# Moving the second MLP's weight tiles 96 bytes along each SBUF partition

## The chip, the cores and the metric

One core of one Trainium2 chip runs the whole program. The metric is the time of one execution on the device, in microseconds (us); the median of several runs is given. A profile is a record of one further execution; its span runs from its first to its last instruction.

## The reference

The input x has 12480 rows of 128 float32 values. The program computes an induced attention and two MLPs one behind the other:

```python
h = mab(inducing, x)          # softmax over 12480 keys, 32 inducing rows
x = mab(x, h)                 # each row of x attends to the 32 rows of h
t = x @ w_in1                 # 128 -> 2048
x = (t * np.cos(t)) @ w_out1  # 2048 -> 128
t = x @ w_in2
return (t * sigmoid(t)) @ w_out2
```

The four weight matrices come as float64 and are narrowed to float32 on the chip.

## The kernel before

A prologue (to 45 us of the span) reads x, computes h, and folds h into the first MLP's first weights: hw = h @ w_in1, so that mlp1_in takes the 32 attention weights of a row in place of the row. From there on a main loop treats 25 blocks, 22 of them of 512 rows of x, the last three of 480, 448 and 288. A block has NJ = 8 units, each of which covers two of the 16 slices of 128 of the hidden 2048.

The order of the work is written out by hand (manual_schedule): each engine executes its instructions in the order of the loop over steps s in main (line 739 on). In a step of the steady state TensorE gets 20 matmuls, of 128 x 128 weights and a moving tile of 512 columns:

- mlp1_in(s), line 761: 2 matmuls, weights hw, moving tile stk, into the PSUM tile h1.
- mlp2_in(s - 11), line 896: 6 matmuls. Weights and moving tile are split into two parts each, hi and lo, and the products wi2_0 x yhi, wi2_1 x yhi and wi2_0 x ylo are added up in the PSUM tile h2; so twice, for two slices.
- mlp2_out(s - 13), by way of down, line 843: 6 matmuls, wo2_0 x hi2 (two slices), wo2_1 x hi2 (two), wo2_0 x lo2 (two), into acc2.
- mlp1_out(s - 1), by way of down, line 843: 6 matmuls of the same form, with wo1_0, wo1_1, hi1 and lo1, into acc1.

So line 843 has the matmuls of both MLPs: in an ordinary step the first six are mlp2_out's and the next six mlp1_out's. In a few steps (held_back) mlp2_in moves behind mlp2_out or behind mlp1_out, since the scores of a later block (line 211) take its PSUM tile h2. The first 12 units of mlp1_out and the first 8 of mlp2_out use unsplit weights (line 853). Beside TensorE, ScalarE takes the cosine (796), the SiLU (911) and the hi part of its result (919), VectorE the product (800) and the parts hi1 and lo1 (807, 833), GpSimd the part lo2 (920).

Each weight tile is split once, in steps 4 to 15 (split, called in the loop): ScalarE writes the hi part (line 191), GpSimd the lo part (line 192). The second MLP's tiles wi2_0, wi2_1, wo2_0 and wo2_1, of 8192 bytes in each partition, come from the pool late, which is opened last (line 719 on), over space that the prologue has given back.

Where the tiles lie in a partition follows from the order and the sizes in which the pools are opened and the tiles asked for; each start is a multiple of 32 bytes. In the built program before:

| tile | first byte | remainder by 128 | remainder by 256 |
|---|---|---|---|
| hw0 to hw3 | 71392 to 77536 | 96 | 224 |
| wo1_0, wo1_1 | 79584, 87776 | 96 | 224 |
| stk | 96000 | 0 | 0 |
| hi1, lo1, hi2, lo2, yhi, ylo (all buffers) | 132992 to 192384 | 0 | 128 |
| wi2_0, wi2_1 | 196480, 204672 | 0 | 128 |
| wo2_0, wo2_1 | 212864, 221056 | 0 | 128 |

A partition ends at byte 229376. The dead tiles of the prologue under wi2 are win, pick, idle, the small ones behind them, e, et and, last, most (212768, 8 bytes); under wo2 there is none.

Of the kernel before, what the change touches and what calls it, by code (L numbers as in the profile page):

```python
# [9 lines left out]
F32 = mybir.dt.float32  # L10
# [12 lines left out]
def tile_induced_attention_then_two_mlps(  # L23
# [36 lines left out]
    P, G, Q = 128, 4, 32  # L60
# [658 lines left out]
    late = ctx.enter_context(tc.tile_pool(name="late", bufs=1, reuse_waits="tile"))  # L719
# [24 lines left out]
    def main(general):  # L744
# [3 lines left out]
        acc1, acc2 = {}, {}  # L748
        ast = {}
        pieces[:] = order[ahead:]  # L750
        wi2 = [late.tile([C, FF], F32R, name=f"wi2_{i}") for i in range(2)]
        wo2 = [late.tile([P, NF, C], F32R, name=f"wo2_{i}") for i in range(2)]
        pair_of.update(in2=wi2, out2=wo2)
# [315 lines left out]
    with tc.If(hot == 0) as arm:  # L1069
        main(False)  # L1070
    stacks = saved
    with arm.Else():
        main(True)
# [34 lines left out]
```

## Time and profile before

| | |
|---|---|
| median of 3 runs | 967.56 us (967.47 to 968.73) |
| profiled execution, its own time | 967.38 us |
| its span | 965.2 us |
| TensorE busy | 951.8 us, 4480 matmul records |
| VectorE busy | 779.3 us |
| ScalarE busy | 691.6 us |
| GpSimd busy | 517.2 us |
| matmuls of line 843 (both down functions) | 53% of the chain that ended last |
| matmuls of line 896 (mlp2_in) | 28% of it |

Busy TensorE means that a matmul was under way; the matmuls are pipelined, and their ends are modelled, so that one overlaps the next in the record. How fast they follow one another is read from their starts, or from differences of their mean durations.

### The profile page before, as it was taken

What the parts mean: (1) busy time and instruction counts of PE and PEld (TensorE: products, weight loads), DVE (VectorE), ACT (ScalarE), POOL (GpSimd) and SP (SyncE); (2) the same over time, 40 slices, a digit from 0 to 9 for tenths busy, and PEclk for the clock granted to TensorE, in tenths of its full rate; (3) what the DMA queues carried; (4) which work ended last, traced back from release to release, by engine and by line L of the source; (5) the groups of instructions that cost most, each with busy time, mean ns of one, the idle gap of its engine ahead of it and who ended that gap; (6) DMA issues with size and microseconds to landing.
All of it is one profiled execution on the core that took longest, in us unless ns stands there. A gap on an engine that the chain in (4) does not pass through costs nothing.

```text
span 965.2 us, 11951 instructions
## 1 busy us (share of the span) xinstructions
PE 951.8 (99%) x4480; PEld 758.0 (79%) x4481; DVE 779.3 (81%) x784; ACT 691.6 (72%) x725; POOL 517.2 (54%) x274
## 2 busy tenths in 40 slices
PE   8899999999999999999999999999999999999997
PEld 5456778888878888878888887888887888888896
DVE  4889888988887988888988887988888888878751
ACT  5687768777668776767777777777767777677774
POOL 3346545654545655554655544655455554555565
PEclk9999999999999999999999999999999999999999
DMA  9341000001010010010010010010010100100001
GB/s 356 112 138 45 6 18 11 14 20 22 2 22 12 12 22 12 12 22 12 12 22 12 12 22 12 12 22 7 17 22 1 22 14 9 21 12 5 13 11 20
DMA packets 65484, 28.19 MB, mean 29 GB/s; under 512 B 54440, under 2 KB 60040, under 8 KB 65416
## 3 DMA queue, kind: packets, MB, share of 16 engines
q1 hardware_dynamic: 64760, 27.24, 10.8%
q8 instruction: 37, 0.61, 0.3%
q14 instruction: 31, 0.25, 0.1%
q10 hardware_dynamic: 656, 0.09, 0.1%
HBM read 14.79 MB, written 6.39 MB: 22 GB/s over the span
## 4 chain that ended last, share of the span: by engine, by line
PE 95%; DMA 2%; DVE 1%; issue 0%; SPq 0%; ACT 0%; POOL 0%; ACTq 0%; POOLq 0%; DVEq 0%
PE acc L843 53%; PE h L896 28%; PE h L761 9%; PE acc L853 4%; DMA x_sb<-in_x_dram 2%; PE s L211 1%; PE pt L392 0%; PE hp L539 0%; SPq L328 0%; PE s L419 0%; DVE et L507 0%; DVE c L800 0%; DVE mx L432 0%; POOL lo L925 0%; PE misc L455 0%
## 5 line engine op out<-in xcount | busy, mean ns | idle before, releaser
L920 POOL TENSOR_TENSOR lo<-s,hi 128x1024 fp32r<-128x1024 f32 (+3 forms) x189 | 446.7, 2364 | 381.0 <-ACT hi L919 359.6
L843 PE MATMUL acc<-hi,wo 128*128 128x512 f32 (+3 forms) x1520 | 406.8, 389 | 0.0
L843 PEld LDWEIGHTS acc<-hi,wo 128*128 128x128 f32 x1520 | 282.5, 188 | 61.5 <-issue 3.7
L800 DVE TENSOR_TENSOR h<-h,c 128x1024 f32<-128x1024 f32 (+3 forms) x188 | 226.1, 1203 | 123.9 <-ACT c L796 123.7
L796 ACT ACTIVATE c<-h,half_pi 128x1024 f32<-128x1024 f32 (+3 forms) x200 | 219.2, 1096 | 146.9 <-PE h L761 146.1
L911 ACT ACTIVATE s<-h 128x1024 f32<-128x1024 f32 (+3 forms) x200 | 201.2, 1006 | 76.6 <-PE h L896 71.8
L896 PE MATMUL h<-yhi,wi 128*128 128x512 f32 (+3 forms) x800 | 244.2, 386 | 0.0
L843 PE MATMUL acc<-lo,wo 128*128 128x512 f32 (+3 forms) x760 | 232.6, 387 | 0.1
L807 DVE CAST hi<-h 128x1024 fp32r<-128x1024 f32 (+3 forms) x188 | 224.9, 1196 | 6.5
L833 DVE TENSOR_TENSOR lo<-h,hi 128x1024 fp32r<-128x1024 f32 (+3 forms) x188 | 223.9, 1191 | 5.7
L919 ACT CAST hi<-s 128x1024 fp32r<-128x1024 f32 (+3 forms) x189 | 195.3, 1033 | 6.1
L896 PEld LDWEIGHTS h<-yhi,wi 128*128 128x128 f32 x800 | 148.8, 188 | 30.7 <-issue 0.5
L843 PEld LDWEIGHTS acc<-lo,wo 128*128 128x128 f32 x760 | 141.9, 188 | 31.2 <-POOL lo L925 0.4
L896 PE MATMUL h<-ylo,wi 128*128 128x512 f32 (+3 forms) x400 | 154.3, 386 | 0.0
L761 PE MATMUL h<-stk,hw 128*128 128x512 f32 (+3 forms) x400 | 126.0, 396 | 1.4 <-ACT stk L704 0.7
L761 PEld LDWEIGHTS h<-stk,hw 128*128 128x128 f32 x400 | 74.1, 188 | 26.8 <-issue 6.5
L896 PEld LDWEIGHTS h<-ylo,wi 128*128 128x128 f32 x400 | 75.1, 188 | 15.2
L877 ACT CAST yhi<-acc 128x512 fp32r<-128x512 f32 (+3 forms) x25 | 14.4, 576 | 15.1 <-PE acc L843 15.0
L943 DVE STREAM_TRANSPOSE o<-acc 128x512 f32<-128x512 f32 (+3 forms) x25 | 17.3, 694 | 9.3 <-PE acc L843 9.3
L853 PE MATMUL acc<-c,wf 128*128 128x512 f32 x48 | 22.5, 591 | 0.0
L878 DVE TENSOR_TENSOR ylo<-acc,yhi 128x512 fp32r<-128x512 f32 (+3 forms) x25 | 16.7, 669 | 5.4 <-ACT yhi L877 5.3
L800 DVE TENSOR_TENSOR c<-h,c 128x1024 f32<-128x1024 f32 x12 | 14.6, 1216 | 2.4 <-ACT c L796 1.9
(133 smaller groups left out, 320.6 us busy)
## 6 DMA issues: line engine op xcount, KB each, us to landing
out_dram<-o SPq DMA_DIRECT2D x80, 64.0 KB, 1.9
x_sb<-in_x_dram SPq DMA_DIRECT2D x8, 512.0 KB, 9.2
raw<-in_moe_w_in_dram SPq DMA_DIRECT2D x8, 512.0 KB, 6.5
raw<-in_moe_w_out_dram SPq DMA_DIRECT2D x8, 512.0 KB, 4.5
stk<-ahi SPq DMA_DIRECT2D x40, 64.0 KB, 2.0
stk<-at SPq DMA_DIRECT2D x40, 64.0 KB, 2.0
x_sb<-in_x_dram SPq DMA_DIRECT2D x3, 256.0 KB, 3.7
x_sb<-in_x_dram SPq DMA_DIRECT2D x2, 320.0 KB
```

What stands on the lines that cost most here:

```text
L761: nc.tensor.matmul(ps[:, a, 0:n], lhsT=hw[f // 4][:, f % 4 * P : (f % 4 + 1) * P], rhs=stacks[b][:, 0:n], start=True, stop=True,)
L796: nc.scalar.activation(cs, h, AF.Sin, bias=half_pi, scale=1.0)
L800: nc.vector.tensor_tensor(cs if whole else h, h, cs, ALU.mult)
L807: nc.vector.tensor_copy(hi[:, :, 0:n], h)
L833: nc.vector.tensor_tensor(lo[:, :, 0:n], h, hi[:, :, 0:n].bitcast(F32), ALU.subtract)
L843: nc.tensor.matmul(acc[:, 0:n], lhsT=wt[:, 2 * j + a, :], rhs=gt[:, a, 0:n], start=(j == 0 and p == 0 and a == 0), stop=(j == NJ - 1 and p ...
L853: nc.tensor.matmul(acc[:, 0:n], lhsT=w[:, 2 * j + a, :], rhs=c[:, a, 0:n], start=(j == 0 and a == 0), stop=(j == NJ - 1 and a == 1),)
L896: nc.tensor.matmul(ps[:, a, 0:n], lhsT=wt[:, fs], rhs=yt[:, 0:n], start=(p == 0), stop=(p == 2),)
L911: nc.scalar.activation(sv, hid2.pop(u)[:, :, 0:n], AF.Silu)
L919: nc.scalar.copy(hv, sv)
L920: nc.gpsimd.tensor_tensor(lv, sv, hv.bitcast(F32), ALU.subtract)
L943: nc.vector.transpose(o.rearrange("p t d -> p (t d)")[:, 0:n], acc2.pop(b)[:, 0:n])
```

## The change

One tile of 24 float32, 96 bytes, that nothing reads or writes is asked of the pool late ahead of the four weight tiles:

```diff
         pieces[:] = order[ahead:]
+        late.tile([P, 24], F32, name="gap")
         wi2 = [late.tile([C, FF], F32R, name=f"wi2_{i}") for i in range(2)]
         wo2 = [late.tile([P, NF, C], F32R, name=f"wo2_{i}") for i in range(2)]
```

So wi2_0 starts at 196576, and the others 96 bytes further on as well: the remainder by 128 becomes 96 and that by 256 becomes 224, which are those of wo1 and hw. The last tile ends at 229344. Nothing else moves.

## Rows read from the trace of the kernel before

**Rows 1.** The page, parts 1 (busy us, share, instructions) and 4 (chain).
```profile
PE 951.8 (99%) x4480; PEld 758.0 (79%) x4481; DVE 779.3 (81%) x784; ACT 691.6 (72%) x725; POOL 517.2 (54%) x274
...
PE 95%; DMA 2%; DVE 1%; issue 0%; SPq 0%; ACT 0%; POOL 0%; ACTq 0%; POOLq 0%; DVEq 0%
```

**Rows 2.** The cores: span and mean granted TensorE clock.
```profile
core 0: 965.2 us, clock 0.998
```

**Rows 3.** Eight steps: stretch, its us, TensorE's busy time and matmuls, clock, DMA.
```profile
506.52:543.26 36.74, 36.74 (x161) 1.00 0.07 15
```

**Rows 4.** The timeline of one ordinary step: start, us, engine, line, operation.
```profile
511.11 0.62 PE L761 MATMUL h<-stk,hw 128*128 128x512 f32 x2
511.57 0.63 PE L896 MATMUL h<-yhi,wi 128*128 128x512 f32 x2
...
512.94 1.07 PE L843 MATMUL acc<-hi,wo 128*128 128x512 f32 x4
...
514.18 1.22 DVE L807 CAST hi<-h 128x1024 fp32r<-128x1024 f32 x1
...
514.30 1.10 PE L843 MATMUL acc<-hi,wo 128*128 128x512 f32 x4
...
515.71 0.39 PE L761 MATMUL h<-stk,hw 128*128 128x512 f32 x1
```

**Rows 5.** The listing by line, 508.74 to 509.6 us: mlp2_out (busy us, mean ns).
```profile
L843 PE MATMUL acc<-hi,wo 128*128 128x512 f32 x3 | 0.8, 389 | 0.0
L843 PE MATMUL acc<-lo,wo 128*128 128x512 f32 x2 | 0.6, 390 | 0.0
```

**Rows 6.** The same listing, 510.11 to 511.0 us: mlp1_out.
```profile
L843 PE MATMUL acc<-hi,wo 128*128 128x512 f32 x3 | 0.9, 398 | 0.0
L843 PE MATMUL acc<-lo,wo 128*128 128x512 f32 x2 | 0.6, 394 | 0.0
```

**Rows 7.** The same listing, 507.37 to 507.80 us: the first matmuls of mlp2_in.
```profile
L896 PE MATMUL h<-yhi,wi 128*128 128x512 f32 x2 | 0.8, 392 | 0.0
L896 PE MATMUL h<-ylo,wi 128*128 128x512 f32 x1 | 0.4, 393 | 0.0
```

**Rows 8.** The same listing, 508.0 to 508.1 us: later matmuls of mlp2_in.
```profile
L896 PE MATMUL h<-yhi,wi 128*128 128x512 f32 x2 | 0.6, 389 | 0.0
```

**Rows 9.** The timeline of a step whose mlp1_out is ahead of mlp2_in.
```profile
156.50 1.10 PE L843 MATMUL acc<-hi,wo 128*128 128x512 f32 x4
...
157.90 0.62 PE L896 MATMUL h<-yhi,wi 128*128 128x512 f32 x2
158.18 1.23 DVE L800 TENSOR_TENSOR h<-h,c 128x1024 f32<-128x1024 f32 x1 [2.16 <-ACT c L796]
...
159.27 0.39 PE L761 MATMUL h<-stk,hw 128*128 128x512 f32 x1
```

**Rows 10.** The listing by line, whole span: writes of wo2's (held) and wo1's (wf) hi parts.
```profile
L191 ACT CAST wo<-held 128x512 fp32r<-128x512 f32 x4 | 2.5, 617 | 0.0
L191 ACT CAST wo<-wf 128x512 fp32r<-128x512 f32 x4 | 2.4, 612 | 0.0
```

**Rows 11.** The listing by line and shape, whole span: matmuls of 512 columns.
```profile
L843 PE MATMUL acc<-hi,wo 128*128 128x512 f32 x1328 | 363.5, 395 | 0.0
L896 PE MATMUL h<-yhi,wi 128*128 128x512 f32 x704 | 219.0, 392 | 0.0
```

**Rows 12.** TensorE's timeline near the end: mlp1_out, then mlp2_out, of 448 columns.
```profile
895.84 0.98 PE L843 MATMUL acc<-hi,wo 128*128 128x448 f32 x4
...
897.08 0.57 PE L761 MATMUL h<-stk,hw 128*128 128x448 f32 x2
...
945.50 0.97 PE L843 MATMUL acc<-hi,wo 128*128 128x448 f32 x4
...
946.72 0.43 PE L896 MATMUL h<-yhi,wi 128*128 128x288 f32 x2
```

## The prediction

> **What bounds the kernel now.** I read the page first: TensorE is busy for 99% of the span, and the chain of waits that ended last lies on it for 95% [rows 1]. The granted clock is 0.998 of full speed, so 2.4 GHz throughout [rows 2]. Eight consecutive steps of the main loop, 160 matmuls, take 36.74 us and TensorE is busy in all of it [rows 3]. So in the main loop a nanosecond added to the spacing of the matmuls is a nanosecond of the run, and one saved there is saved until another engine's work becomes the longer; VectorE, the next, has 779.3 us in the span [rows 1]. The question is then only what sets the spacing of the matmuls.
>
> Next the timeline of one step [rows 4]. It has 20 matmuls of 512 columns: two of mlp1_in, six of mlp2_in, six of mlp2_out, six of mlp1_out. From start to start the groups take 511.57 - 511.11 = 0.46, 512.94 - 511.57 = 1.37, 514.30 - 512.94 = 1.36 and 515.71 - 514.30 = 1.41 us. mlp2_out and mlp1_out are the same function on the same shapes with the same kinds of operands, and yet one needs 0.05 us more. The listing by line, cut to those stretches, sharpens this. Its mean durations carry a modelled end, some 162 ns past the next start (389 ns beside 1.36 us / 6 = 227 ns), which drops out in differences. mlp2_out runs at 389 and 390 ns [rows 5], mlp1_out at 398 and 394 [rows 6]. mlp2_in runs at 392 and 393 in its first three matmuls [rows 7] and 389 after them [rows 8].
>
> What differs? The moving tiles (hi1, lo1, hi2, lo2, yhi, ylo) all start 0 bytes past a multiple of 128, and the second MLP's weights do too; wo1 and hw start 96 past one. The spacing follows the weights, not the moment: in the step from 154.59 us, in which the score work puts mlp1_out ahead of mlp2_in, mlp1_out again takes 157.90 - 156.50 = 1.40 us although VectorE had then stood idle for 2.16 us, and mlp2_in right behind it takes 159.27 - 157.90 = 1.37 us while VectorE works [rows 9]. In the ordinary step mlp1_out has VectorE beside it [rows 4]. Both times its price is the same. So neighbours on other engines don't make it.
>
> **The change, part by part.** *The unused tile.* It issues no instruction and no DMA, on no queue; no wait is added, so nothing is queued behind one. The four tiles still lie over the same dead tiles of the prologue (win to et, and most), so their first writers wait for the same releases. The last one ends 32 bytes below the end of a partition. Cost: zero; there is nothing that would need cover.
>
> *The writes of the moved tiles* (line 191 on ScalarE, line 192 on GpSimd). ScalarE writes to the tiles that move take 617 ns; those to wo1, which already lies at the new offset, take 612 [rows 10]. Eight such writes at a difference of -5 to +5 ns are 0.04 us, beside the matmuls. Zero.
>
> *The reads of the moved tiles by TensorE.* This is the whole price. After the change each matmul of the second MLP has weights 96 bytes past a multiple of 128 and a moving tile at 0, as mlp1_out has now. I take its rate. The two shown mlp1_out groups take 1.40 and 1.41 us, so 1.40 / 6 = 233 to 1.41 / 6 = 235 ns a matmul.
>
> - mlp2_out: from 389.4 to about 396.4 mean ns (three at 398 and two at 394 [rows 6] against three at 389 and two at 390 [rows 5]), that is 7 ns. Count: 1328 hi of 512 columns are listed under line 843 [rows 11], and by the code half as many lo, 664. mlp1_out has 164 units of six, 984, which leaves 1008. 1008 x 7 ns = 7.1 us.
> - mlp2_in: now (392.3 + 389) / 2 = 390.7; with the group's first matmul counted, mlp1_out has some 5 ns more (1.40 - 1.37 = 0.03 us in six). Count 704 yhi [rows 11] and half as many ylo: 1056 x 5 ns = 5.3 us.
> - The second mlp1_in matmul, behind which the first wi2 weights are loaded: no row by itself. Between 0 and 7 ns, 176 times, 0 to 1.2 us; I take the middle, 0.5.
> - Units of fewer columns: at 448, mlp1_out takes 897.08 - 895.84 = 1.24 us and mlp2_out 946.72 - 945.50 = 1.22 [rows 12], so 0.02 us a group, 16 groups, 0.3 us. Others: I take zero.
>
> Sum 7.1 + 5.3 + 0.5 + 0.3 = 13.2 us. The profiled execution took 967.38 us (span 965.2), 0.2 below the median of 967.56; 967.4 + 13.2 = **980.6 us**. All of it lies on the path, because TensorE has no idle time to give. No other engine is late next: they get 0.07 us more per step, and wait longer for TensorE.
>
> *Bounds.* Nearest from below: the moved weights cost only what the three unsettled matmuls of mlp2_in show, 392.3 mean ns [rows 7]. That is 2.9 x 1008 + 1.6 x 1056 = 4.6 us, 972.0. From above: all at 398, the slowest row of mlp1_out [rows 6], 8.6 x 1008 + 7.3 x 1056 = 16.4 us, with the small terms at 1.5 985.3. The middle is taken since it is the mean of the only group that has the new combination.
>
> **The rivals.** *No change (967.5 us).* The slow rate belongs to something of mlp1_out other than the address of its weights: its accumulator, acc1, lies in another PSUM bank than acc2. For it: each of the two groups has its own bank, and no row separates bank from weights. Against it: mlp2_in runs at both rates in the same bank h2 [rows 7, 8], and hw, at wo1's offset, writes h1, and its pair takes 0.46 us [rows 4], 230 ns each, above mlp2_out's 227. That the tiles don't move would also end here; the sizes (96 bytes, then four times 8192, pool opened last) speak against it.
>
> The Trainium skill, SBUF — State Buffer, section "SBUF: two separate sides", gives TensorE its own read ports, with a second independent one for the weights; by that rule the place of the weights is without effect and the time would stay at 967.5 us. The trace doesn't agree well. TensorE: Matmul & The Clock Gate, section "Back-to-back issue gap", gives 512 / 2.4 + 2.5, an estimate of 216 ns for such a matmul by itself; here they lie at 227 to 236, so weight loads and matmuls cost one another something.
>
> *Faster (about 959 us).* What is slow is not an offset but the change from one offset to another between successive weights, and after the change mlp2_in, mlp2_out and mlp1_out have one offset. It decides if a run of matmuls with equal offsets settles at 389 wherever that offset is. Then mlp1_out gets mlp2_out's rate, 0.04 us a step, and the first three of mlp2_in gain 3 x 3.3 ns, 0.01 us: 0.05 x 170 steps = 8.5 us. For it: mlp2_in is slow just behind mlp1_in and settles after three. Against it: mlp1_out doesn't settle within its six matmuls (the three behind its first run at 398, the two after them at 394 [rows 6]); and mlp2_in right behind mlp1_out needs no more than 1.37 us [rows 9], so a change of offset by itself isn't dear.
>
> **How the numbers follow.** Slower, as summed: 0.80. No change: 0.11. Faster: 0.09. A difference under 0.2% (1.9 us) can't be told from no change here. The forecast's own range is 972 to 986 and holds most of its 0.80; the range given reaches down to 967, so that it takes in the case of no change, and leaves out the faster case and the forecast's tails.
>
> **What would show it.** Right: mlp2_out at 395 to 398 mean ns in the listing by line, a step of 4.66 us or more instead of 4.59, mlp1_out unchanged at 394 to 398, the same number of instructions, and no new wait ahead of lines 191 and 192. Wrong: mlp2_out still at 389 (then it is the bank or the time), or mlp1_out at 389 too (then it was the change of offset). The size is wrong if six matmuls in a row are too few to show where a longer run at the new offset settles: then the rate changes along the 12 to 18 matmuls that come behind mlp1_in.

## The result, and the profile after

The changed kernel takes 981.34 us (median of 4 runs, 979.73 to 981.91) beside 967.67 us (967.47 to 968.73) for the one before: a ratio of 1.0139, 95% interval 1.0126 to 1.0152. The forecast was 980.6.

The page and the cores first; the line of part 1 answers to [rows 1], the core's to [rows 2]. The span here is that of the profiled execution, which took 981.91 us.

```profile
PE 965.3 (99%) x4481; PEld 760.4 (78%) x4481; DVE 779.8 (80%) x784; ACT 691.5 (71%) x725; POOL 517.2 (53%) x274
```
```profile
core 0: 979.7 us, clock 0.998
```

VectorE, ScalarE and GpSimd are busy for as long as before, to 0.5 us, with the same counts; the granted clock is the same. Only TensorE has more: 965.3 for 951.8 us. (One matmul record more is in the trace; the program has as many as before.) The time went into the spacing of the matmuls.

The timeline of one ordinary step, which answers to [rows 4]; lines stand one further down in the changed kernel.

```profile
514.06 0.63 PE L762 MATMUL h<-stk,hw 128*128 128x512 f32 x2
514.53 0.62 PE L897 MATMUL h<-yhi,wi 128*128 128x512 f32 x2
...
515.92 1.10 PE L844 MATMUL acc<-hi,wo 128*128 128x512 f32 x4
...
517.32 1.10 PE L844 MATMUL acc<-hi,wo 128*128 128x512 f32 x4
...
518.73 0.63 PE L762 MATMUL h<-stk,hw 128*128 128x512 f32 x2
```

From start to start: mlp1_in 0.47 us (before 0.46), mlp2_in 1.39 (1.37), mlp2_out 515.92 to 517.32, 1.40 (1.36), mlp1_out 1.41 (1.41, and 1.40 in [rows 9]). A step takes 4.67 us for 4.60. mlp2_out now runs as mlp1_out does.

The listing by line and shape over the whole span, matmuls of 512 columns (busy us, mean ns): after, and then the rows of before that did not stand ahead of the prediction.

```profile
L844 PE MATMUL acc<-hi,wo 128*128 128x512 f32 x1328 | 367.9, 399 | 0.0
L897 PE MATMUL h<-yhi,wi 128*128 128x512 f32 x704 | 221.4, 396 | 0.0
L844 PE MATMUL acc<-lo,wo 128*128 128x512 f32 x664 | 209.5, 397 | 0.0
L897 PE MATMUL h<-ylo,wi 128*128 128x512 f32 x352 | 139.7, 397 | 0.0
L762 PE MATMUL h<-stk,hw 128*128 128x512 f32 x352 | 114.7, 407 | 1.3 <-ACT stk L704 0.7 <-DVE c L801 0.6
```
```profile
L843 PE MATMUL acc<-lo,wo 128*128 128x512 f32 x664 | 206.8, 392 | 0.0
L896 PE MATMUL h<-ylo,wi 128*128 128x512 f32 x352 | 137.7, 391 | 0.0
L761 PE MATMUL h<-stk,hw 128*128 128x512 f32 x352 | 113.2, 403 | 1.4 <-ACT stk L704 0.7 <-DVE c L800 0.6
```

Less the busy times of [rows 11], 363.5 and 219.0 us, and of the rows above, that is 4.4 us (hi) and 2.7 (lo) for the two down functions, 2.4 and 2.0 for mlp2_in and 1.5 for mlp1_in: 13.0 us in all, with the same counts. The spans differ by 979.7 - 965.2 = 14.5. TensorE's timelines, before and then after, show where the rest lies: the first mlp1_in, and the last group of the run.

```profile
44.93 1.21 PE L761 MATMUL h<-stk,hw 128*128 128x512 f32 x4 [0.73 <-ACT stk L704]
...
957.79 0.82 PE L843 MATMUL acc<-lo,wo 128*128 128x288 f32 x2
```
```profile
45.73 0.72 PE L762 MATMUL h<-stk,hw 128*128 128x512 f32 x2 [0.73 <-ACT stk L704]
...
971.70 0.79 PE L844 MATMUL acc<-lo,wo 128*128 128x288 f32 x2
```

From one to the other it is 912.86 us before and 925.97 after, 13.1 us more, which the listing accounts for. 0.8 us lie ahead of it, where the prologue's transposes waited 1.3 us for x in place of 0.6, and 0.6 us behind it. The change touches neither, and the same program, run again with two tags traded (below), starts its first mlp1_in at 44.33 us.

### The profile page after: what moved, and what is told of

Same layout as the page of the kernel before. It is cut to its first block, busy times and chain, and to the rows that moved or that the text cites. A ratio compares the mean times of both kernels' runs of the same rounds, so it can differ in the third digit from the quotient of the medians.

```text
span 979.7 us, 11952 instructions
## 1 busy us (share of the span) xinstructions
PE 965.3 (99%) x4481; PEld 760.4 (78%) x4481; DVE 779.8 (80%) x784; ACT 691.5 (71%) x725; POOL 517.2 (53%) x274
## 4 chain that ended last, share of the span: by engine, by line
PE 96%; DMA 2%; DVE 1%; issue 0%; ACT 0%; SPq 0%; POOL 0%; ACTq 0%; POOLq 0%; DVEq 0%
PE acc L844 53%; PE h L897 28%; PE h L762 9%; PE acc L854 4%; DMA x_sb<-in_x_dram 2%; PE s L211 1%; PE hp L539 0%; PE pt L392 0%; PE s L419 0%; DVE et L507 0%; SPq L328 0%; DVE c L801 0%; DVE mx L432 0%; PE misc L455 0%; POOL lo L926 0%
## 5 line engine op out<-in xcount | busy, mean ns | idle before, releaser
L844 PE MATMUL acc<-hi,wo 128*128 128x512 f32 (+3 forms) x1520 | 411.2, 392 | 0.0
L844 PE MATMUL acc<-lo,wo 128*128 128x512 f32 (+3 forms) x760 | 235.2, 390 | 0.1
L897 PE MATMUL h<-ylo,wi 128*128 128x512 f32 (+3 forms) x400 | 156.3, 391 | 0.0
L392 PEld LDWEIGHTS pt<-ident,x_sb 128*128 128x128 f32 x98 | 11.2, 147 | 6.9 <-PE hp L539 3.1
```

The source lines that it names most:

```text
L844: nc.tensor.matmul(acc[:, 0:n], lhsT=wt[:, 2 * j + a, :], rhs=gt[:, a, 0:n], start=(j == 0 and p == 0 and a == 0), stop=(j == NJ - 1 and p ...
L897: nc.tensor.matmul(ps[:, a, 0:n], lhsT=wt[:, fs], rhs=yt[:, 0:n], start=(p == 0), stop=(p == 2),)
```

## The experiments

A tile's offset is its first byte's remainder by 256; the distance is the weights' offset less the moving tile's, again by 256. Before, the distance was 96 in mlp1_out, 224 in mlp1_in and 0 in the second MLP; the change made it 96 there too. In every kernel that follows the same arithmetic is done on the same values, and what differs, if anything, is places.

### The unused tile smaller

The edit of gap32, ahead of wi2:

```diff
+        late.tile([P, 8], F32, name="gap")
```

And that of gap64:

```diff
+        late.tile([P, 16], F32, name="gap")
```

> The second MLP's weights start 32 bytes past a multiple of 128, the moving tiles at 0. If the spacing follows the distance in bytes between weights and moving tile (my theory), 32 is another distance than 0 and 96; neither has a row yet. If any distance but 0 keeps the matmuls from settling, mlp2_out goes from 389 to about 396 mean ns and the run to 979 to 982 us, as at 96. If the slow rate is due to an accumulator's bank or to the moment, or if only 96 is slow, 967.5 us. If what matters is that all weights have one offset, this kernel has two, as before: 967.5 us as well.

> The second MLP's weights start 64 bytes past a multiple of 128. If the distance by 128 counts, slow as at 96, 979 to 982 us with mlp2_out near 396 mean ns. If only the place by 64 counts (wo1 and the changed tiles lie 32 past a multiple of 64, before none did), then 64 is as good as 0: 967.5 us and mlp2_out at 389.

Measured: gap32 978.60 us, ratio 1.0121 (1.0104 to 1.0138); gap64 977.09 us, 1.0098 (1.0081 to 1.0115). The listing by line of gap64:

```profile
L844 PE MATMUL acc<-hi,wo 128*128 128x512 f32 x1328 | 365.8, 397 | 0.0
L844 PE MATMUL acc<-lo,wo 128*128 128x512 f32 x664 | 208.9, 396 | 0.0
```

Both are slower than before, a little less than at 96 (397 and 396 ns here, 398 and 396 in gap32, against 399 and 397). gap32 came out 0.4 us and gap64 2 us under my lower end. So 96 is nothing special, and the place by 64 doesn't decide: a distance of 64 is dear as well.

### The first MLP's weights at a multiple of 256

```diff
+    flag = persist.tile([1, 1], I32, name="flag")
     hw = [persist.tile([P, FF // 4], F32R, name=f"hw{i}") for i in range(4)]
     wo1 = [persist.tile([P, NF, C], F32R, name=f"wo1_{i}") for i in range(2)]
-    flag = persist.tile([1, 1], I32, name="flag")
```

> The tile flag is asked for ahead of hw, so that hw and wo1 start at a multiple of 128 (and of 256), as the second MLP's weights do by 128; all else stays. My theory: mlp1_out drops from 396 to 389 mean ns, 984 matmuls by 6.7 ns = 6.6 us, the unsettled first three of mlp2_in 176 x 10 ns = 1.8 us and the second mlp1_in at most 1 us: 958 to 961 us. If a period of 256 counts, wo1 now stands at 128 from its moving tile by 256 and need not gain: 964 to 970. Bank or moment: 967.5, and mlp1_out stays at 396.

Measured: 973.50 us, ratio 1.0069 (1.0052 to 1.0086). No branch of the expectation held: it got slower. TensorE's timeline of one of its steps:

```profile
513.96 0.63 PE L761 MATMUL h<-stk,hw 128*128 128x512 f32 x2
514.43 0.64 PE L896 MATMUL h<-yhi,wi 128*128 128x512 f32 x2
...
515.83 1.08 PE L843 MATMUL acc<-hi,wo 128*128 128x512 f32 x4
...
517.21 1.10 PE L843 MATMUL acc<-hi,wo 128*128 128x512 f32 x4
...
518.60 0.63 PE L761 MATMUL h<-stk,hw 128*128 128x512 f32 x2
```

mlp1_out, from 517.21, takes 1.39 us, hardly less than the 1.40 to 1.41 of before. So a start at a multiple of 128 isn't what makes a tile fast, for wo1 has it now: its distance by 256 is 128. And mlp2_in rose from 1.37 to 1.40 us and mlp2_out from 1.36 to 1.38, although none of their tiles was moved. A matmul's rate therefore depends on more than its own two tiles. Over the 129 ordinary steps of this trace the matmuls come back to 227 ns from start to start only with the fourth of mlp2_out, so the reading is that the slow matmuls ahead of them in the stream cost them something.

### The accumulators' tags traded

```diff
-                acc1[b] = psa.tile([P, 512], F32, tag="acc1" if b else "acc2", name="acc1")
+                acc1[b] = psa.tile([P, 512], F32, tag="acc2" if b else "acc1", name="acc1")
...
-                acc2[b] = psa.tile([P, 512], F32, tag="acc2", name="acc2")
+                acc2[b] = psa.tile([P, 512], F32, tag="acc1", name="acc2")
```

> acc1 and acc2 trade their PSUM banks, no tile of the SBUF moves. My theory: no change, 967.5 us, mlp1_out at 396 and mlp2_out at 389 mean ns. If the bank makes the slow rate, the two trade their rates: mlp2_out 396, mlp1_out 389, and the sum stays about the same, so the rates decide and not the time.

The edit trades the tags under which acc1 and acc2 are asked for, and not the banks: in both built programs acc1 of the first block and every acc2 lie in bank 6 and acc1 of the later blocks in bank 7, and the two programs have the same instructions with the same addresses. So this is the kernel before, run again, and not the trade that the expectation speaks of.

Measured: 967.36 us, ratio 1.0000 (0.9991 to 1.0010). That is how closely two sets of runs of one program agree; it says nothing on the banks. The rival of the banks falls by other runs. With every accumulator where it was, the change took mlp2_out from 1.36 to 1.40 us, and all_at_128, which follows, takes mlp1_out from 1.40 to 1.36.

### Everything at one offset: 128, then 224

The edit of all_at_128:

```diff
+    flag = persist.tile([1, 1], I32, name="flag")
+    m2 = persist.tile([P, KT, 1], F32, name="m2")
+    sm = persist.tile([P, KT, 1], F32, name="sm")
     hw = [persist.tile([P, FF // 4], F32R, name=f"hw{i}") for i in range(4)]
...
-    flag = persist.tile([1, 1], I32, name="flag")
...
-        "m2": persist.tile([P, KT, 1], F32, name="m2"),
-        "sm": persist.tile([P, KT, 1], F32, name="sm"),
+        "m2": m2,
+        "sm": sm,
```

In all_at_224 flag stays, and m2 and sm are asked for ahead of stk, with an unused tile of 96 bytes that moves all that follows:

```diff
+    m2 = persist.tile([P, KT, 1], F32, name="m2")
+    sm = persist.tile([P, KT, 1], F32, name="sm")
+    persist.tile([P, 24], F32, name="gap")
     stk = persist.tile([P, 2, W], F32R, name="stk")
```

> flag, m2 and sm are asked for ahead of hw, so that hw, wo1 and stk start 128 past a multiple of 256, where the second MLP's weights and the moving tiles already lie. My theory, mended after the run with wo1 at 0: the distance between weights and moving tile counts by 256, not by 128, and at distance 0 the matmuls settle at 227 ns. Then all 20 of a step do: mlp1_out from 234 to 227 ns, 984 x 6.7 = 6.6 us, mlp2_in from 229 to 227, 2.3 us, mlp1_in about 0.4 us, 957 to 960 us. If only a multiple of 128 counted, this would be as slow as the run with wo1 at 0, 973.5 us. If the first MLP's rate has nothing to do with places, 967.5 us or more.

> Every weight tile and every moving tile of the main loop, stk too, starts 224 past a multiple of 256 (96 past one of 128). If the distance counts, this is the kernel with all of them at 128 once more, 957 to 960 us. If a start at a multiple of 128 is what makes a tile fast, nothing is there any longer: 980 us or more.

Measured: all_at_128 957.69 us, ratio 0.9907 (0.9891 to 0.9924); all_at_224 958.33 us, 0.9906 (0.9890 to 0.9923). TensorE's timeline of all_at_128:

```profile
514.46 0.61 PE L763 MATMUL h<-stk,hw 128*128 128x512 f32 x2
514.91 0.62 PE L898 MATMUL h<-yhi,wi 128*128 128x512 f32 x2
...
516.27 1.07 PE L845 MATMUL acc<-hi,wo 128*128 128x512 f32 x4
...
517.63 1.07 PE L845 MATMUL acc<-hi,wo 128*128 128x512 f32 x4
...
518.99 0.62 PE L763 MATMUL h<-stk,hw 128*128 128x512 f32 x2
```

All three groups of six take 1.36 us and mlp1_in 0.45; a step is 4.53 us. The listing of both kernels, all_at_128 first:

```profile
L845 PE MATMUL acc<-hi,wo 128*128 128x512 f32 x1328 | 358.5, 392 | 0.0
L845 PE MATMUL acc<-lo,wo 128*128 128x512 f32 x664 | 204.6, 389 | 0.0
```
```profile
L846 PE MATMUL acc<-hi,wo 128*128 128x512 f32 x1328 | 358.6, 392 | 0.0
L846 PE MATMUL acc<-lo,wo 128*128 128x512 f32 x664 | 204.6, 389 | 0.0
```

The two can't be told apart, though in all_at_224 no weight and no moving tile of the main loop starts at a multiple of 64. The offset itself does nothing; the distance decides.

### The moving tiles and the second MLP's weights shifted together

```diff
+    pad = ctx.enter_context(tc.tile_pool(name="pad", bufs=1, reuse_waits="tile"))
+    pad.tile([P, 24], F32, name="gap")
     u1 = ctx.enter_context(tc.tile_pool(name="u1", bufs=2, reuse_waits="tile"))
```

> An unused tile of 96 bytes ahead of the working tiles moves hi1, lo1, hi2, lo2, yhi, ylo and the second MLP's weights 96 bytes on; hw, wo1 and stk stay. So the second MLP's weights start 96 past a multiple of 128, as in the changed kernel, but their moving tiles do too, and wo1's moving tiles now have its offset. If the distance counts: mlp2_out stays at 227 ns, mlp1_out falls from 234 to 227, only mlp1_in keeps its distance, 959 to 963 us. If the weights' own offset counts: mlp1_out stays at 234 and the second MLP goes there, 979 to 982 us.

Measured: 961.24 us, ratio 0.9941 (0.9925 to 0.9958).

```profile
516.94 0.63 PE L763 MATMUL h<-stk,hw 128*128 128x512 f32 x2
517.40 0.63 PE L898 MATMUL h<-yhi,wi 128*128 128x512 f32 x2
517.87 0.39 PE L898 MATMUL h<-ylo,wi 128*128 128x512 f32 x1
518.10 0.62 PE L898 MATMUL h<-yhi,wi 128*128 128x512 f32 x2
...
518.78 1.07 PE L845 MATMUL acc<-hi,wo 128*128 128x512 f32 x4
```

The second MLP's weights lie at the very bytes of the changed kernel, and yet this one is 19 to 20 us faster. Their moving tiles went with them. mlp2_in's first three matmuls still take 518.10 - 517.40 = 0.70 us and its last three 0.68: mlp1_in, alone with a distance other than 0, unsettles what comes behind it. all_at_224 differs from this kernel in the place of stk and of tiles that these matmuls don't read: 961.24 - 958.33 = 2.9 us for that pair of matmuls and what it does to those behind it, or 3.7 us from the first mlp1_in to the last matmul in the two traces.

### The change under study, made to the kernel with all at 128

To the edit of all_at_128 comes that of the change:

```diff
+        late.tile([P, 24], F32, name="gap")
         wi2 = [late.tile([C, FF], F32R, name=f"wi2_{i}") for i in range(2)]
```

> The kernel with all tiles at 128, and in it the change under study alone: the second MLP's weights lie 96 bytes further on. If each matmul's rate hangs on its own distance: mlp1_out stays at 227 ns, the second MLP goes to 234, 958 + 14 = 971 to 974 us. If the slow second MLP unsettles the first as well, as the run with wo1 at 0 unsettled the second, 975 to 981 us. If the change of distance between successive weights were what costs, it would be the slowest of all, above 981 us.

Measured: 973.68 us, 16.0 above all_at_128 (957.69); against the kernel before 1.0070 (1.0053 to 1.0087). The listing, 516.37 to 517.3 us (mlp2_out), and 517.78 to 518.6 us (mlp1_out):

```profile
L846 PE MATMUL acc<-hi,wo 128*128 128x512 f32 x3 | 0.9, 396 | 0.0
L846 PE MATMUL acc<-lo,wo 128*128 128x512 f32 x2 | 0.6, 396 | 0.0
```
```profile
L846 PE MATMUL acc<-hi,wo 128*128 128x512 f32 x3 | 0.8, 390 | 0.0
L846 PE MATMUL acc<-lo,wo 128*128 128x512 f32 x2 | 0.6, 389 | 0.0
```

The two MLPs have traded the rates of [rows 5, 6], one at 396 and the other at 390. This kernel has a change of offset between successive weights in each step, and is 7 to 8 us faster than the changed kernel, whose MLP weights all have one offset. That takes away the faster rival: what is dear is the distance to the moving tile, not a change from one weight tile to the next.

### A distance of 256

```diff
-    half_pi = persist.tile([P, 1], F32, name="half_pi")
-    quarter = persist.tile([P, 1], F32, name="quarter")
-    s_w = persist.tile([P, 1], F32, name="s_w")
...
-    flag = persist.tile([1, 1], I32, name="flag")
     stk = persist.tile([P, 2, W], F32R, name="stk")
+    half_pi = persist.tile([P, 1], F32, name="half_pi")
+    quarter = persist.tile([P, 1], F32, name="quarter")
+    s_w = persist.tile([P, 1], F32, name="s_w")
+    flag = persist.tile([1, 1], I32, name="flag")
```

> The small tiles half_pi, quarter, s_w and flag are asked for behind stk, so that hw, wo1 and stk start 96 bytes nearer to the partition's start (stk 128 nearer): 128 past a multiple of 512, where the moving tiles hi1 and lo1 and the second MLP's tiles start 384 past one. wo1 is then 256 from its moving tiles, stk 0 from hw. If the distance counts by 256, this is the kernel with all at 128 again: mlp1_out 227 ns, 957 to 960 us. If it counts by 512 or more, mlp1_out stays slow, 233 ns, and the second MLP may lose its rate too: 965 to 974 us.

Measured: 957.78 us, ratio 0.9899 (0.9883 to 0.9916).

```profile
L843 PE MATMUL acc<-hi,wo 128*128 128x512 f32 x1328 | 358.5, 392 | 0.0
L843 PE MATMUL acc<-lo,wo 128*128 128x512 f32 x664 | 204.4, 389 | 0.0
```

A distance of 256 is as good as 0, while one of 128 wasn't: of the distance in these runs, the remainder by 256 is what counts.

## Why the prediction was right

**The bound.** TensorE is the path before and after, and the spacing arrived: 13.0 us by the busy times of its matmuls of 512 columns, 13.1 from the first mlp1_in to the last group. The same held the other way, in the kernels at 957 to 958 us. The range given, from 967 us on, would have held a run without any change too; what bears the forecast out is mlp2_out's step from 1.36 to 1.40 us in six matmuls, the rate of mlp1_out.

**The price of the reads.** Line 843 has 7.1 us more. By the starts of the matmuls some 6.3 of it is mlp2_out's, which was sized 7.1. mlp2_in was sized 5.3 us and has 2.4 + 2.0 = 4.4. Both a little high.

**Two small terms were too low, and one too high.** mlp1_in, where I took 0.5 between 0 and 1.2, has 1.5 us. mlp1_out, at zero in the sum, rose by some 0.9 us. The units of 448 columns, sized 0.3 us, cost nothing: mlp2_out there takes 1.21 us after, and 1.22 in [rows 12], and the listing of all hi matmuls of 448 columns, before and after, has 366 and 365 ns.

```profile
957.30 0.97 PE L844 MATMUL acc<-hi,wo 128*128 128x448 f32 x4
...
958.51 0.42 PE L897 MATMUL h<-yhi,wi 128*128 128x288 f32 x2
```
```profile
L843 PE MATMUL acc<-hi,wo 128*128 128x448 f32 x64 | 15.7, 366 | 0.0
L844 PE MATMUL acc<-hi,wo 128*128 128x448 f32 x64 | 15.6, 365 | 0.0
```

**What failed in the reasoning, and cancelled in the sum.** That mlp1_out costs nothing more rests on the idea that each matmul has its rate from its own pair of tiles. wo1_at_0 shows that this is not so: matmuls whose tiles stayed put lost 0.02 to 0.03 us in six. The prediction marked the dear tiles by their start, 96 bytes past a multiple of 128; the mark is the distance from weights to moving tile by 256. Both gave the same forecast for this change, since the remainders by 256 that the front matter lists match as well. That the sum of 13.2 us met the 13.1 measured on this stretch so closely is luck: three terms were together some 2 us too high and two some 2 us too low.

**The writes and waits.** ScalarE's and GpSimd's busy times are unchanged, and the writes of line 191 to the moved tiles take 615 ns (617 in [rows 10]):

```profile
L191 ACT CAST wo<-held 128x512 fp32r<-128x512 f32 x4 | 2.5, 615 | 0.0
```

**The rivals.** Bank: shown wrong by the result and by all_at_128, in which the rates of mlp2_out and mlp1_out changed while their banks did not; no run traded the banks. The moment, or other engines: [rows 9] spoke against it, and all_at_128 confirms it, since there mlp1_out sits beside the same engines' work at 1.36 us. Change of offset: shown wrong by mlp1_at_0_mlp2_at_96, and by the changed kernel itself, in which the weights of the MLP stages have one offset and none is fast.

The Trainium skill, SBUF — State Buffer, section "SBUF: two separate sides", by whose two independent read ports of TensorE the place of the weights would be without effect, does not fit these runs: the same instructions take 957.7 to 981.3 us as the places vary.

**What stays open.** Why the distance counts isn't shown. The next weights load while a matmul streams its moving tile. In the trace of before, the load for the matmul of 508.35 us starts at 508.12, together with the matmul ahead of it:

```profile
508.12 0.39 PE L896 MATMUL h<-ylo,wi 128*128 128x512 f32 x1
508.12 0.41 PEld L843 LDWEIGHTS acc<-hi,wo 128*128 128x128 f32 x2
508.35 0.39 PE L843 MATMUL acc<-hi,wo 128*128 128x512 f32 x1
```

So the two reads lie side by side, and that they meet in the memory is an argument from the numbers, no observation.

Nor did an experiment tell whether the weights' partner is their own moving tile or the one that streams while they load. Three rows of the listing speak for the second. In wo1_at_0 the last two matmuls of mlp2_out (516.92 to 516.96 and 517.15 to 517.2 us) both have distance 0 from weights to moving tile. But beside the last of them wo1's weights load, at 128 from the lo2 that it streams, and of the two it alone is slow: over the 129 ordinary steps the next matmul starts 226 ns behind the first of them and 233 behind the second. In shift_moving (521.45 to 521.48 us) hw's weights load beside the last matmul of mlp1_out. They are at 224 from their own stk and at 0 from the lo1 that streams, and that matmul is as fast as any. The rows stand in this order:

```profile
L843 PE MATMUL acc<-lo,wo 128*128 128x512 f32 x1 | 0.4, 389 | 0.0
L843 PE MATMUL acc<-lo,wo 128*128 128x512 f32 x1 | 0.4, 396 | 0.0
L845 PE MATMUL acc<-lo,wo 128*128 128x512 f32 x1 | 0.4, 389 | 0.0
```

## What to carry to other kernels

Where TensorE is the path and matmuls alternate with weight loads, compare the spacing of matmuls of equal shape across lines, and where it differs, list the first bytes of weights and moving tiles. In these kernels weights and moving tiles at the same remainder by 256 ran 3% closer (227 against 234 ns at 512 columns); moving a few small tiles was enough to get it for all of them, and took the kernel before from 967 to 957.7 us. A small tile asked for between big ones can undo it for all that follow. Look the places up in the built program: the traded tags above moved nothing.

## What the runs showed that was not expected

- The kernel before was itself 1% off: only the second MLP had distance 0. The best version, all_at_128, is 957.69 us (0.9907) and wo1_at_256 957.78 us (0.9899); they and all_at_224 can't be told apart.
- A partial repair can be worse than none: distance 0 for the second MLP and 128 for mlp1_out (973.5 us) is slower than 0 and 96 (967.2 us in the same comparison). That kernel moved hw too: mlp1_in's distance by 256 went from 224 to 0.
- The price depends on the number of columns. At 448 columns the distance of 96 cost mlp2_out nothing measurable (1.21 us for 1.22 in the group shown), while at 512 it cost 0.04 us in six.
